# Attention and MLP on one core: the second MLP product by Strassen's scheme for eight of nine chunks of 512 tokens

## The chip, the core and the metric

The kernel runs on one core of a Trainium2 chip. The metric is the device time of one execution in microseconds (us); lower is better. Engines are named as in the profile: PE is TensorE (matmuls), PEld its weight loads, DVE VectorE, ACT ScalarE, POOL GpSimd, SP the sync engine, whose queue issues most DMAs.

## What is computed

The reference is attention over 8 batches of 8 heads (576 tokens, head size 64), in which scores more than tau below the maximum of their row are dropped, followed by an MLP on the 4608 tokens of 512 features:

```python
def _moe_ref(x, w_in, w_out) -> np.ndarray:
    h = x @ w_in
    sp = np.where(h > 20.0, h, np.log1p(np.exp(np.minimum(h, 20.0))))
    g = h * np.tanh(sp)
    return (g @ w_out).astype(np.float32)
```

`w_in` is 512 x 2048, `w_out` 2048 x 512. The gate h * tanh(softplus(h)) is one ACT instruction (Mish). The change concerns `g @ w_out`, the second product.

## The kernel before, in words

Matmuls take float32r operands, and each full-precision operand is split in two: an upper half (a copy into float32r, by ACT) and a lower half (the operand minus that copy, by DVE or POOL). A product is the sum of three matmuls: upper x upper, upper x lower, lower x upper. The weights arrive as 64-bit words and are decoded (class `Decode`): two conversions on ACT (`first`), clamp, shift and sign on DVE, `add` on POOL, then the upper half on ACT and the lower on DVE or POOL.

The first part of `attention_moe` (to line 655) runs attention tile by tile, with the first MLP product (`gemm1`) of the batch before it mixed in. `gemm1` takes 384 matmuls of 288 tokens a batch, in units of 12 that fill one PSUM bank (128 rows of h, 288 tokens); a copy by ACT or DVE takes each out, and four go to DRAM (`hd`) in one DMA.

Lines 657 to 799 are the first product of the last batch, 32 units (`u`). Beside it the first quarter of `w_out` is decoded in pieces of 256 columns (`PACE`), and h of the first tokens is loaded and gated (`GATES`, `GATES1`).

From line 800 on is the second product. Tokens go in chunks: 256, eight of 512, and 256. For each chunk and each 128 of the 512 output features (`d`), 48 matmuls with the chunk's tokens as moving columns run into one PSUM bank: 16 blocks of 128 hidden rows (`f`), three matmuls each (line 851). DVE copies the bank out (line 854), SP stores it (line 855). `make_g` makes the operand of the next chunk in pieces of 1024 elements: load, Mish (line 679), upper half on ACT (line 683), lower half on DVE (line 684). The rest of `w_out` is decoded during the first two chunks.

Every engine gets its instructions in the order in which the program makes them.

## Time and profile before

| | us |
|---|---|
| median of 3 runs | 1372.05 (1371.4 to 1372.26) |
| the profiled execution: its span | 1370.5 |
| second product, first matmul to end of span | 968.4 to 1370.5 |

The span is the time from the first to the last instruction of one profiled execution; the median of the runs is 1.55 us above it. In a group's row stand line, engine, operation, output<-input, shapes, count, busy time in all and mean ns of one, and behind the last bar the engine's idle time ahead of them and who ended it. A timeline row has start, duration, engine, line, operation; in brackets the idle time before it and the engine waited for. Line 94 is a helper that records operations, so names of tiles tell them apart there.

### The profile page before, as it was taken

To read this page: it belongs to the slowest core of one execution; us is meant where nothing else is said; L and a number is where in the kernel's file an instruction comes from. 1 tells how busy PE (TensorE), PEld (TensorE's weight loads), DVE (VectorE), ACT (ScalarE), POOL (GpSimd) and SP (SyncE) were. 2 spreads that over 40 slices of the span, in tenths; PEclk is the share of its full clock that TensorE was granted. 3 is DMA by queue.
4 is the path that set the end of the run, shared out by engine and by line. 5 is a ranking of instruction groups with operands and counts; after the bars stand their busy time and mean duration, and the time that the engine had idled before them with its cause. 6 is when DMAs were issued, how large, how long until landed. Compare 5 with 4: busy or idle time off the path is not lost.

```text
span 1370.5 us, 27694 instructions
## 1 busy us (share of the span) xinstructions
PE 1352.6 (99%) x8839; PEld 1225.3 (89%) x8839; DVE 1001.6 (73%) x2976; ACT 943.0 (69%) x2106; POOL 771.8 (56%) x1115
## 2 busy tenths in 40 slices
PE   9998899999999999999999999999999999999999
PEld 7555889999999999999999999999887888888888
DVE  6999999999999999999999999957874332232210
ACT  5878788888888888888888888856555543443210
POOL 5778888778788787887887878633460000000000
PEclk9999999999999999999999999999999999999999
DMA  5333323333333233332332323128655553543310
GB/s 152 98 98 107 114 80 114 108 96 103 101 99 115 89 120 93 111 107 97 103 112 88 124 90 110 60 88 277 196 164 151 153 148 102 143 131 102 93 52 23
DMA packets 126017, 154.64 MB, mean 113 GB/s; under 512 B 23472, under 2 KB 109488, under 8 KB 125872
## 3 DMA queue, kind: packets, MB, share of 16 engines
q1 hardware_dynamic: 124720, 148.16, 36.1%
q10 hardware_dynamic: 1152, 4.72, 0.9%
q8 instruction: 70, 1.15, 0.4%
q14 instruction: 75, 0.61, 0.1%
HBM read 105.64 MB, written 47.19 MB: 112 GB/s over the span
## 4 chain that ended last, share of the span: by engine, by line
PE 84%; DVE 5%; ACT 4%; DMA 2%; issue 2%; POOL 2%; SPq 1%; ACTq 0%; DVEq 0%; POOLq 0%
PE h L94 25%; PE o L851 23%; PE s L94 13%; PE y L94 12%; PE tp L94 9%; PE t L94 1%; DVE st L94 1%; DVE g L94 1%; DVE p L94 1%; DVE dec L94 1%; POOL w2l L157 1%; DMA ht<-hd 1%; DMA g<-hd 1%; ACT e L94 1%; DMA g<-w_out 1%
## 5 line engine op out<-in xcount | busy, mean ns | idle before, releaser
L851 PE MATMUL o<-g,w2h 128*128 128x512 f32 (+1 forms) x1280 | 363.9, 370 | 0.8 <-DVE g L684 0.8
L94 PE MATMUL h<-xh,w1h 128*128 128x288 f32 x1024 | 302.8, 296 | 1.1 <-ACT hst L94 0.6
L94 PE MATMUL h<-xh,w1l 128*128 128x288 f32 x1024 | 302.6, 296 | 0.0
L94 PE MATMUL h<-xl,w1h 128*128 128x288 f32 x1024 | 302.6, 295 | 0.0
L94 POOL TENSOR_SCALAR p<-p,st 128x576 f32<-128x576 f32 x288 | 243.8, 846 | 58.2 <-DVE st L94 33.8
L851 PEld LDWEIGHTS o<-g,w2h 128*128 128x128 f32 x1280 | 231.7, 188 | 43.7 <-DVE g L684 1.1
L94 PE MATMUL s<-k,q 128*128 128x288 f32 (+1 forms) x1280 | 255.2, 324 | 8.2 <-DVE p L94 7.9
L94 DVE SCALAR_TENSOR_TENSOR p<-s,st,e 128x576 f32<-128x576 f32 x288 | 235.1, 816 | 20.5 <-ACT e L94 11.0
L94 ACT ACTIVATE e<-s,st 128x576 f32<-128x576 f32 x288 | 214.2, 744 | 36.0 <-DVE st L94 30.4
L851 PE MATMUL o<-g,w2l 128*128 128x512 f32 (+1 forms) x640 | 236.2, 369 | 0.0
L94 DVE TENSOR_REDUCE st<-s 128x1 f32<-128x576 f32 x288 | 216.7, 752 | 2.6 <-PE s L94 2.5
L94 PEld LDWEIGHTS s<-k,q 128*128 128x128 f32 (+1 forms) x1280 | 182.7, 190 | 38.1 <-DVE p L94 23.6
L94 DVE TENSOR_TENSOR lo<-tp,hi 128x512 fp32r<-128x512 f32 (+1 forms) x280 | 174.7, 632 | 49.2 <-ACT hi L94 42.5
L94 PEld LDWEIGHTS h<-xh,w1h 128*128 128x128 f32 x1024 | 193.1, 189 | 1.9 <-ACT hst L94 1.1
L94 PEld LDWEIGHTS h<-xh,w1l 128*128 128x128 f32 x1024 | 193.0, 188 | 0.0
L94 PEld LDWEIGHTS h<-xl,w1h 128*128 128x128 f32 x1024 | 192.9, 188 | 0.0
L94 PE MATMUL tp<-ident,p 128*128 128x128 f32 x1152 | 174.4, 274 | 3.3 <-DVE lo L94 2.1
L94 ACT CAST hi<-tp 128x512 fp32r<-128x512 f32 (+1 forms) x280 | 149.7, 545 | 36.1 <-PE tp L94 33.1
L684 DVE TENSOR_TENSOR g<-ht,g 128x1024 fp32r<-128x1024 f32 (+1 forms) x60 | 68.6, 1153 | 137.0 <-ACT g L683 137.0
L94 PEld LDWEIGHTS tp<-ident,p 128*128 128x128 f32 x1152 | 138.9, 140 | 13.4 <-issue 5.4
L679 ACT ACTIVATE ht<-ht 128x1024 f32<-128x1024 f32 (+1 forms) x60 | 60.2, 1003 | 115.5 <-DMA ht<-hd 111.0
L851 PEld LDWEIGHTS o<-g,w2l 128*128 128x128 f32 x640 | 120.3, 188 | 21.3
(87 smaller groups left out, 2223.0 us busy)
## 6 DMA issues: line engine op xcount, KB each, us to landing
hd<-hst SPq DMA_DIRECT2D x56, 576.0 KB, 3.4
r<-q SPq DMA_DIRECT2D x120, 160.0 KB, 2.3
r<-k SPq DMA_DIRECT2D x120, 160.0 KB, 2.3
ht<-hd SPq DMA_DIRECT2D x52, 288.0 KB, 3.2
r<-v SPq DMA_DIRECT2D x56, 160.0 KB, 2.3
dec<-w_in SPq DMA_DIRECT2D x32, 256.0 KB, 2.8
out_t<-ost SPq DMA_DIRECT2D x32, 256.0 KB, 2.9
g<-w_out SPq DMA_DIRECT2D x48, 128.0 KB, 3.0
```

What stands on the lines that cost most here:

```text
L94: made = method(*args, **kwargs)
L157: engine.tensor_tensor(self.lo, fv(self.a), fv(self.hi), ALU.subtract)
L679: nc.scalar.activation(ht, ht, AF.Mish)
L684: engine.tensor_tensor(gl, ht, fv(gh), ALU.subtract)
L851: nc.tensor.matmul(o[:, :m], a, b, start=n == 0, stop=n == 3 * NF - 1)
```

## The change

The first 512 tokens (chunk 0) are multiplied as before, but with all four output blocks open at once: 8 groups, one for each pair of hidden blocks (j and j + 8), of 24 matmuls with 512 columns. The other 4096 tokens go in eight chunks of 512 by Strassen's scheme in Winograd's form. The output of a chunk is a 2 x 2 block matrix (two halves of the features, two of the tokens), as is each pair of hidden blocks; seven products of quarter size take the place of eight. A chunk has 8 groups of 7 products x 2 x 3 = 42 matmuls of 256 columns, in seven PSUM banks. So there are 72 groups (`NG`), numbered n; group n of chunk c is j = n - 8c.

- `load_z` loads h of a group (two DMAs), four quarters of 256 tokens.
- `combine` applies Mish (ACT, 1024 elements) and, for Strassen's chunks, makes three more quarters: one subtraction of 512 elements on DVE, then two of 256 on POOL, the second of which needs the first.
- `split_z` makes the upper half `gh` (ACT) and the lower half `gl` (DVE) of the seven quarters, 1792 elements each. `gh` and `gl` have three buffers.
- `sums_w` and `split_w` make the sums of the weight's quarters for chunks 1 to 8, beside chunk 0's matmuls.
- `leave` adds the seven products into four output quarters: one copy on ACT and seven additions on DVE out of PSUM, and four stores.
- `compose`, `upper_w`, `lower_w` decode the weight in pieces of 1024 elements, all of it beside the last batch of the first product, a piece every 4 units.
- h lies in DRAM in blocks of 256 tokens, so each store of it (`store`) is two DMAs; three weight loads and conversions move into the last steps of attention. The buffers of the first weight's decode, and the DMA scratch, are placed anew.

Its core, cut:

```diff
+        def compose(j):
...
+            nc.vector.tensor_scalar(fv(b), fv(top), TOP_MAX, -TOP_MAX, ALU.min, ALU.max)
+            nc.vector.tensor_scalar(a, b, 3, 0x7FFFFFF8, ALU.logical_shift_left, ALU.bitwise_and)
+            nc.vector.scalar_tensor_tensor(b, b, 0x80000000, a, ALU.bitwise_and, ALU.bitwise_or)
+            nc.gpsimd.tensor_tensor(b, b, low, ALU.add)
...
+        def combine(n):
+            if n < NG:
+                y = z[n]
+                nc.scalar.activation(y[:, :4], y[:, :4], AF.Mish)
+                if n >= NJ:
+                    nc.vector.tensor_tensor(
+                        y[:, 4:6], y[:, :1].to_broadcast([P, 2, QT]), y[:, 1:3], ALU.subtract
+                    )
+                    nc.gpsimd.tensor_tensor(y[:, 6], y[:, 1], y[:, 5], ALU.subtract)
+                    nc.gpsimd.tensor_tensor(y[:, 7], y[:, 6], y[:, 3], ALU.subtract)
+
+        def split_z(n):
+            if n < NG:
+                home = homes[("er", "wl", "wl")[n % 3]]
+                gs[n] = [home.tile([P, 7, QT], F32R, name=f"g{m}", tag=f"g{m}{n % 3}") for m in "hl"]
+                y = z[n][:, :4] if n < NJ else z.pop(n)[:, 1:]
+                to = [x[:, :4] if n < NJ else x for x in gs[n]]
+                nc.scalar.copy(to[0], y)
+                nc.vector.tensor_tensor(to[1], y, fv(to[0]), ALU.subtract)
...
+                    if NT <= g < NT + 3:
+                        convert(g - NT)
...
-                ost = wl.tile([P, NC], F32, name="ost", bufs=2)
-                nc.vector.tensor_copy(ost[:, :m], o[:, :m])
-                nc.sync.dma_start(out[d * P:(d + 1) * P, CHUNKS[c]:CHUNKS[c + 1]], ost[:, :m])
...
+        for n in range(NG):
+            c, j = divmod(n, NJ)
+            if n < NJ:
+                sums_w(n)
+            for i in range(n + 1 + (n > NJ + 1), n + 2 + (n > NJ)):
+                split_z(i)
+            if n < NJ:
+                split_w(n)
+            for i in range(n + 2 + (n > NJ), n + 3 + (n >= NJ)):
+                if i > 2:
+                    combine(i)
+            for i in range(n + 3 + (n >= NJ), n + 4 + (n >= NJ - 1)):
+                if i > 4:
+                    load_z(i)
...
+            for k, (wi, gi) in enumerate(PRODUCTS):
+                o = banks[k].rearrange("p (n t) -> p n t", t=QT)
+                w, at = (wa[j], (0, 2, 3)[wi]) if wi < 3 else (ws[j], wi - 3)
+                for b in range(2):
+                    cols = slice(at * QT + b * P, at * QT + (b + 1) * P)
+                    for i, (x, y) in enumerate(((0, 0), (0, 1), (1, 0))):
+                        nc.tensor.matmul(
+                            o[:, b], w[x][:, cols], gs[n][y][:, gi],
+                            start=j == b == i == 0, stop=j == NJ - 1 and b == 1 and i == 2,
+                        )
+                if j == NJ - 1:
+                    leave(k, c, o)
```

The order that this makes of DVE's queue in the steady part. Before, between two output copies (`ost`), DVE has only lower halves of 1024 elements, each of which waits for ACT's upper half:

```order
L684 TENSOR_TENSOR g_17501<-ht_17509,g_17501 128x1024
L684 TENSOR_TENSOR g_17516<-ht_17517,g_17516 128x1024
L684 TENSOR_TENSOR g_17516<-ht_17524,g_17516 128x1024
L854 COPY ost_17595<-o_17546 128x512
L684 TENSOR_TENSOR g_17531<-ht_17532,g_17531 128x1024
```

Now, at the end of a Strassen chunk (`z` written at 512 elements is the subtraction of `combine`, `c` the additions of `leave`):

```order
L91 TENSOR_TENSOR gl_16692<-z_16593,gh_16691 128x1792
L91 TENSOR_TENSOR z_16646<-z_16646 128x512
L91 TENSOR_TENSOR gl_16745<-z_16646,gh_16744 128x1792
L91 TENSOR_TENSOR z_16699<-z_16699 128x512
L91 TENSOR_TENSOR c_16769<-o_16374,c_16761 128x512
L91 TENSOR_TENSOR c_16777<-o_16375,c_16769 128x512
L91 TENSOR_TENSOR c_16785<-o_16376,c_16777 128x512
L91 TENSOR_TENSOR c_16769<-o_16376,c_16769 128x512
L91 TENSOR_TENSOR c_16769<-o_16377,c_16769 128x512
L91 TENSOR_TENSOR c_16777<-c_16777,o_16378 128x512
L91 TENSOR_TENSOR c_16761<-o_16379,c_16761 128x512
L91 TENSOR_TENSOR gl_16814<-z_16699,gh_16813 128x1792
```

The subtraction of a group stands behind `gl` of the group before it and ahead of its own `gl`; seven additions stand between the two once a chunk. ACT's queue there, with the engines whose semaphores each instruction waits for in brackets:

```order
L91 ACTIVATE z_16593<-z_16593 128x1024 [waits DMAHW6_49,DMAHW5_49]
L91 CAST gh_16691<-z_16593 128x1792 [waits DVE_49,PE_49,Pool_49]
L91 ACTIVATE z_16646<-z_16646 128x1024 [waits DMAHW7_49,DMAHW0_49]
L91 CAST gh_16744<-z_16646 128x1792 [waits DVE_49,PE_49,Pool_49]
L91 ACTIVATE z_16699<-z_16699 128x1024 [waits DMAHW2_49,DMAHW1_49]
```

`gh` of a group now waits for POOL's two subtractions, on an engine that has nothing to do in this part of the kernel before. The second place is DVE's queue from the end of the last first-product batch into chunk 0. Before, decoding and gating alternate with copies of h in small pieces:

```order
L94 TENSOR_TENSOR g_15361<-ht_15407,g_15360 128x1024
L94 COPY hst_15555<-h_15591 128x288
L94 TENSOR_SCALAR g_15359<-g_15359 128x256 x2
L94 SCALAR_TENSOR_TENSOR g_15359<-g_15359 128x256
```

Now the last piece of the weight (`w2l7`), the sums of its first piece and `gl` of group 1 (`gl_16025`):

```order
L91 TENSOR_SCALAR s_15941<-w_15747 128x1024
L91 TENSOR_SCALAR a_15940<-s_15941 128x1024
L91 SCALAR_TENSOR_TENSOR s_15941<-s_15941,a_15940 128x1024
L91 COPY hst_15962<-h_15949 128x288
L91 COPY hst_15962<-h_15980 128x288
L91 TENSOR_TENSOR w2l7_15994<-s_15941,w2h7_15939 128x1024
L91 TENSOR_TENSOR z_15766<-s_15414 128x256 x2
L91 TENSOR_TENSOR z_15766<-z_15766,s_15414 128x256
L91 TENSOR_TENSOR z_15766<-s_15414,z_15766 128x256
L91 TENSOR_TENSOR gl_16025<-z_15792,gh_16024 128x1024
```

The operand of chunk 0's second group stands behind the whole decode of the weight, which before lay partly beside the first two chunks.

## Prediction

> **What bounds the kernel now.** I read the page first: how long each engine is busy, and the chain that ended last.

> ```profile
> span 1370.5 us, 27694 instructions
> PE 1352.6 (99%) x8839; PEld 1225.3 (89%) x8839; DVE 1001.6 (73%) x2976; ACT 943.0 (69%) x2106; POOL 771.8 (56%) x1115
> PE 84%; DVE 5%; ACT 4%; DMA 2%; issue 2%; POOL 2%; SPq 1%; ACTq 0%; DVEq 0%; POOLq 0%
> ```

> TensorE (PE) is busy 99% of the span and owns the chain, so only fewer or cheaper matmuls shorten this kernel, as long as they are fed. Next the busy time by stage: attention's end, the start of the second product, and its steady part (columns: window, length, PE, weight loads, DVE, ACT, POOL, granted clock, DMA share, GB/s).

> ```profile
> 903.00:911.00 8.00, 8.00 (x62) 7.95 (x61) 2.72 (x7) 4.42 (x12) 1.88 (x3) 1.00 0.18 74
> 968.40:1026.00 57.60, 57.60 (x347) 51.31 (x346) 46.56 (x76) 31.92 (x74) 35.88 (x44) 1.00 0.51 156
> 1026.00:1370.50 344.50, 340.47 (x1577) 282.35 (x1575) 92.80 (x99) 120.26 (x123) 0.00 (x0) 1.00 0.39 110
> ```

> In the steady part DVE works 27% and ACT 35%, POOL not at all: there the other engines only convert the hidden values ahead of PE. The table of PE's waits has one wait in the whole second product:

> ```profile
> PE o L851 <- DVE g L684: 0.8, 1, 0.8
> ```

> The pace of the matmuls is read from when results leave (a matmul's own duration overlaps its neighbours'). Timeline of PE at the product's start, and of DVE near its end:

> ```profile
> 968.41 0.40 PE L851 MATMUL o<-g,w2h 128*128 128x256 f32 x2
> ...
> 1333.69 0.69 DVE L854 COPY ost<-o 128x512 f32<-128x512 f32 x1 [10.29 <-PE o L851]
> 1344.68 0.69 DVE L854 COPY ost<-o 128x512 f32<-128x512 f32 x1 [10.30 <-PE o L851]
> ...
> 1367.26 0.42 DVE L854 COPY ost<-o 128x256 f32<-128x256 f32 x1 [5.26 <-PE o L851]
> ```

> 48 matmuls of 512 columns take 10.99 us, 0.229 us each. The last 192, of 256 columns, take 22.58 us, 0.1176 each. Half the columns cost a little over half.

> **The matmuls: what the change saves.** Before, the product runs from 968.4 to 1367.3, 398.9 us. After, chunk 0 has 192 matmuls of 512 columns (43.9 us, 5.5 per group of 24), and each of eight chunks has 8 groups of 42 matmuls of 256: 4.94 us a group, 39.5 a chunk, 316.1 in all. Together 360.0: 38.9 us less, if PE never waits.

> [...]

> **The round that feeds a group.** Does PE stay fed? These groups of instructions have the forms that the new code uses (line, engine, operation, form, count, busy, mean ns):

> ```profile
> L684 DVE TENSOR_TENSOR g<-ht,g 128x1024 fp32r<-128x1024 f32 x52 | 63.2, 1224 | 124.1 <-ACT g L683 124.1
> L684 DVE TENSOR_TENSOR g<-ht,g 128x512 fp32r<-128x512 f32 x8 | 5.5, 692 | 12.9 <-ACT g L683 12.9
> L683 ACT CAST g<-ht 128x1024 fp32r<-128x1024 f32 x52 | 54.0, 1049 | 35.3 <-PE o L851 34.1
> L683 ACT CAST g<-ht 128x512 fp32r<-128x512 f32 x8 | 4.9, 620 | 12.4 <-PE o L851 12.2
> L679 ACT ACTIVATE ht<-ht 128x1024 f32<-128x1024 f32 x52 | 55.1, 1060 | 103.9 <-DMA ht<-hd 99.4 <-DVE ost L854 4.4
> L94 DVE TENSOR_TENSOR lo<-tp,hi 128x512 fp32r<-128x512 f32 x224 | 153.6, 686 | 40.1 <-ACT hi L94 34.8
> L94 POOL TENSOR_TENSOR k<-r,k 128x320 fp32r<-128x320 f32 x120 | 104.6, 877 | 9.9 <-ACT k L94 6.7
> ```

> Drawn out in a straight line to 1792 elements, ACT's upper half (gh) takes 1.049 + 768 x 0.838 ns = 1.69 us and DVE's lower half (gl) 1.224 + 768 x 1.04 ns = 2.02. The DVE subtraction of 512 takes 0.69, Mish 1.06. By engine a group costs ACT 2.75, DVE 2.71 and POOL about 1.5, each well under PE's 4.94. But they stand in one line. DVE's queue holds gl of group m, then the subtraction of m+1, then gl of m+1. The subtraction of m+1 therefore starts after gl of m; POOL's two need it; ACT's gh of m+1 needs POOL's; gl of m+1 needs gh. No two of these overlap, and each round makes one group.

> How much lies between engines is read from the timelines: DVE to POOL, POOL to ACT, ACT to DVE.

> ```profile
> 966.96 0.43 DVE L94 SCALAR_TENSOR_TENSOR g<-g 128x256 uint32<-128x256 uint32 x1
> 967.52 0.74 POOL L94 TENSOR_TENSOR g<-g 128x256 uint32<-128x256 uint32 x1 [4.18 <-DVE g L94]
> ...
> 943.37 0.81 POOL L94 TENSOR_TENSOR g<-g 128x256 uint32<-128x256 uint32 x1 [0.74 <-DVE g L94]
> 944.21 0.41 ACT L94 CAST w2h<-g 128x256 fp32r<-128x256 f32 x1 [1.14 <-POOL g L94]
> ...
> 963.72 1.05 ACT L94 CAST g<-ht 128x1024 fp32r<-128x1024 f32 x1
> 964.80 1.23 DVE L94 TENSOR_TENSOR g<-ht,g 128x1024 fp32r<-128x1024 f32 x1 [2.35 <-ACT g L94]
> ```

> The hops are 0.13, 0.03 and 0.03; POOL's 256 elements take 0.74 to 0.81. The round: gl 2.02 (less 0.07 by which the next DVE instruction starts early, below) + 0.69 + 0.13 + 2 x 0.76 + 0.03 + 1.69 + 0.03 = 6.04. POOL's second subtraction waits for its first, which no row prices: 0 to 0.3. I take **6.1 us**, with ends of 5.75 (shorter POOL and DVE starts) and 6.5 (0.07 more at each of five handovers). That is more than 4.94, so once the lead is used up, PE waits 1.1 to 1.2 us in every group.

> Is DVE's order really kept? In the trace it is:

> ```profile
> 939.22 1.22 DVE L94 TENSOR_TENSOR g<-ht,g 128x1024 fp32r<-128x1024 f32 x1 [4.53 <-ACT g L94]
> 940.37 0.45 DVE L94 COPY hst<-h 128x288 f32<-128x288 f32 x1
> ...
> 939.75 0.38 ACT L94 COPY hst<-h 128x288 f32<-128x288 f32 x1
> ```

> ACT's copy is of the bank that PE filled after the one that DVE copies here, and PE needs 12 matmuls for a bank, at least 1.4 us at 0.1176. So the bank of DVE's copy was full by 938.3, while DVE idled (4.53 us, until 939.22) for the instruction queued ahead of that copy. The copy then started 1.15 after an instruction of 1.22: the 0.07 above. [...]

> **Chunk edges.** At the end of a chunk seven DVE additions out of PSUM (0.69 each, as lo<-tp,hi; 4.8, with waits on each other 4.9) are queued between the subtraction and gl. 3.4 us of that lies beside POOL and gh; **1.5** is added, at seven edges 10.5 (0.8 to 2.6 each). Products of the next chunk wait for the banks that the additions empty (0.7 + 4.9 + 0.7 = 6.3 us after gl of its second group), so its first group ends late; but gh of three groups further, which overwrites that group's tiles, is due two rounds and the 1.5 less gl and gh after the same moment, 10 us, so this goes no further. On SP's queue four output DMAs stand ahead of the next load.

> ```profile
> L855 SPq DMA_DIRECT2D out_t<-ost x40: 332/351/467, 1013.8 to 1367.7; - x40
> ```

> They delay it by 4 x 0.35 = 1.4 us behind the last addition; it lands some 3 us later and is wanted two rounds on: nothing, and 1.4 an edge if that cover is gone. Mish of a group lies beside gl of the group before (1.06 of 2.02), its loads four rounds ahead: nothing. The new places of buffers and scratch put no instruction on any queue.

> **Entry.** The decode of the weight now goes by 1024 elements: clamp, shift and sign on DVE, add on POOL, upper on ACT, lower on DVE, with the next clamp behind the lower.

> ```profile
> 917.60 1.57 POOL L94 TENSOR_TENSOR xl<-x,xh 128x288 fp32r<-128x288 f32 x2 [0.55 <-ACT xh L94]
> 945.60 0.69 DVE L94 CAST g<-g 128x1024 fp32r<-128x1024 f32 x1 [1.67 <-DMA ht<-hd]
> 943.15 0.42 DVE L94 TENSOR_TENSOR w2l<-g,w2h 128x256 fp32r<-128x256 f32 x1
> ```

> By the POOL rows (0.74 at 256, 0.877 at 320) its 1024 take 2.35. A turn: clamp 0.69 to 1.2 (strided input, unseen), shift 0.69, sign 1.2, hop 0.13, add 2.35, upper 1.05, lower 1.15: 7.3 to 7.8, say 7.5. The first add waits for POOL's xl, done at 919.2; lower 0 ends at 923.8, two copies at 924.6, and seven turns later lower 7 at 977.1. Behind it stand four sums of 0.42 and gl of group 1: 980.0. PE wants that at 968.4 + 5.5 = 973.9: **6.1 us** of waiting (4 to 9). Then sums, gl and sl take DVE 4.1 us a group against 5.5, and PE runs free to the end of chunk 0. With eight PSUM banks in turn I expect no stop of PE inside the first product.

> **Attention.** Each store of h becomes two DMAs and three conversions of 2.1 us on ACT come into its last steps, where it works 4.4 of 8 us; their cover is that idle time, and an ACT copy that is late by one conversion can hold PE's bank up to about 1 us. I take 1, from -1 to 3.

> **The sum.** Chunk 0 ends at 968.4 + 1 + 43.9 + 6.1 = 1019.4. The lead, counted from there: DVE copies out the last bank (0.7), gl of 9 ends at 3.0, two subtractions at 4.2, POOL's pairs at 5.2 and 6.7, gh of 10 at 6.9, gl of 10 at 9.0 and of 11 at 11.0, and a round later that of 12 at 17.0. PE wants 9 to 12 at 4.9, 9.9, 14.8 and 19.8; at 1.2 us a group the lead is gone by group 15. gl of the last group, 59 rounds after group 12: 17.0 + 59 x 6.1 + 10.5 = 387.4, and 4.9 for its matmuls: 1411.7. The tail:

> ```profile
> out_t<-ost SPq DMA_DIRECT2D x32, 256.0 KB, 2.9
> out_t<-ost SPq DMA_DIRECT2D x8, 128.0 KB, 1.9
> ```

> From the last copy's start to the end it took 3.2; the last piece is now 256 KB (+1.0) and an addition of 0.69 for a copy of 0.42 (+0.3): 4.5. Span 1416.2. The median of the three runs, 1372.05, is 1.55 above the profiled span, so **1418 us**.

> **Rivals.** (1) PE stays the bound and the kernel is faster: a round under 4.94 us. 1418 - 387.4 - 4.9 + 316.1 = **1342**. It speaks for it that no engine's own work reaches 4.94; against it that all seven legs come from rows and stand in line. A round of 5.3 already equals 1372 ((1418 - 1372)/59 = 0.78 less). Chance 0.10.
> (2) PE's clock falls. It was granted 1.00 in every stage quoted, where PE was busy at least 98%; no row shows it with a wait in every group. At half clock a group takes 9.9 us, over the round, and the time is 1342 + 316 = **1658**. [...] Chance 0.04.

> **How the numbers follow.** The forecast has 0.86. The round's ends move it by 59 x -0.35 = -21 and 59 x 0.4 = +24, the other terms by 5 to 8 either way, less often together: 1395 to 1445, which leaves out both rivals and about 0.06 of the forecast. Within 0.2% (2.7 us, about what measurement can tell here) only a round of 5.3 ends: 0.01. Faster 0.10, slower 0.89.

> **What would show it.** Right: in the steady part gh starts every 6.1 us, DVE idles before gl for ACT and ACT before gh for POOL, PE's waits there are for gl and 70 to 80 us in sum (392 - 316), PE busy near 80%. Wrong: PE waits for nothing after chunk 0, or gh starts every 4.9 us; or a clock under 1.00 there.

## The result, and the profile after

The changed kernel takes **1421.8 us** (median of 4 runs, 1421.1 to 1421.8); the kernel before, beside it, 1372.0. The ratio is 1.0365 (95% interval 1.035 to 1.0381): slower by 50 us, 3.8 over the 1418 of the forecast and inside its range. The page of the profile after, its span, busy times and chain:

```profile
span 1420.0 us, 29648 instructions
PE 1345.4 (95%) x9799; PEld 1264.5 (89%) x9799; DVE 1102.4 (78%) x3018; ACT 990.0 (70%) x2052; POOL 837.0 (59%) x1191
issue 20%; POOL 6%; PE 3%; DVE 1%; ACT 0%; DMA 0%; POOLq 0%; DVEq 0%; ACTq 0%
```

The shares of the chain add up to 31% of the span: it was followed back to 979.7 us only, so it holds the second product alone and can't be set against the 84% of before as it stands. Of its 440 us PE has 40, nearly all in chunk 0; before, the last 321 us of matmuls were PE's in one piece. What owns the rest can't be read from this row: "issue" is the time that the chain could not give to anyone, here between POOL's pairs. The timelines show it. One round of the steady part (DVE, then POOL and ACT; the brackets have the wait and who ended it):

```profile
1099.59 2.02 DVE L91 TENSOR_TENSOR gl<-z,gh 128x1792 fp32r<-128x1792 f32 x1 [3.39 <-ACT gh L91]
1101.54 0.68 DVE L91 TENSOR_TENSOR z<-z 128x512 f32<-128x512 f32 x1
1105.60 2.03 DVE L91 TENSOR_TENSOR gl<-z,gh 128x1792 fp32r<-128x1792 f32 x1 [3.38 <-ACT gh L91]
...
1102.30 1.54 POOL L91 TENSOR_TENSOR z<-z 128x256 f32<-128x256 f32 x2 [4.46 <-DVE z L91]
...
1103.88 1.69 ACT L91 CAST gh<-z 128x1792 fp32r<-128x1792 f32 x1 [3.35 <-POOL z L91]
```

Follow the starts: gl 1099.59, subtraction 1101.54, POOL's pair 1102.30, gh 1103.88, gl of the next group 1105.60. Each begins within 0.1 us of the end of the one before it, none lies beside another, and the round is **6.01 us** (6.04 worked out, 6.1 taken). All three engines idle over half of it and none is late by its own work.

At a chunk edge the seven additions stand ahead of gl; it starts 7.32 us after the one before, 1.3 more than a round:

```profile
1123.61 2.02 DVE L91 TENSOR_TENSOR gl<-z,gh 128x1792 fp32r<-128x1792 f32 x1 [3.35 <-ACT gh L91]
...
1126.15 3.67 DVE L91 TENSOR_TENSOR c<-o,c 128x512 f32<-128x512 f32 x5
...
1130.93 2.01 DVE L91 TENSOR_TENSOR gl<-z,gh 128x1792 fp32r<-128x1792 f32 x1
```

PE's longest waits (what it waited for, sum in us, times, longest; all lie in the steady part but one of the 19 for gl, 0.5 us at the entry), and the window of the steady part (length, PE, weight loads, DVE, ACT, POOL, clock, DMA share, GB/s):

```profile
PE o L91 <- ACT c L91: 31.4, 7, 4.5
PE o L91 <- DVE gl L91: 12.3, 19, 0.8
```

```profile
1050.00:1410.00 360.00, 315.46 (x2471) 308.31 (x2469) 184.97 (x166) 157.10 (x124) 85.05 (x116) 0.93 0.32 100
```

That is not the picture that the forecast drew: PE is busy 88%, not 80%, its largest wait is for a PSUM bank at the chunk's edge and not for gl, and the granted clock is 0.93. A table of waits read alone would name the banks. The experiments ask whether PE, its clock or its banks have any part in the 50 us.

### The profile page after: what moved, and what is told of

It is laid out like the page before. It is cut to its first block, busy times and chain, and to the rows that moved or that the text cites. A ratio compares the mean times of both kernels' runs of the same rounds, so it can differ in the third digit from the quotient of the medians.

```text
span 1420.0 us, 29648 instructions
## 1 busy us (share of the span) xinstructions
PE 1345.4 (95%) x9799; PEld 1264.5 (89%) x9799; DVE 1102.4 (78%) x3018; ACT 990.0 (70%) x2052; POOL 837.0 (59%) x1191
## 5 line engine op out<-in xcount | busy, mean ns | idle before, releaser
L91 POOL TENSOR_TENSOR z<-z 128x256 f32<-128x256 f32 x128 | 94.3, 737 | 332.1 <-DVE z L91 319.9
L91 DVE TENSOR_TENSOR gl<-z,gh 128x1792 fp32r<-128x1792 f32 (+1 forms) x72 | 140.7, 1956 | 191.6 <-ACT gh L91 191.5
L91 ACT CAST gh<-z 128x1792 fp32r<-128x1792 f32 (+1 forms) x72 | 116.4, 1619 | 224.5 <-POOL z L91 210.1
L91 DVE SCALAR_TENSOR_TENSOR p<-s,st,e 128x576 f32<-128x576 f32 x288 | 235.0, 816 | 20.3 <-ACT e L91 10.5
L91 PE MATMUL o<-gh,sh 128*128 128x256 f32 x512 | 152.6, 298 | 32.7 <-ACT c L91 31.4
L91 PE MATMUL o<-gh,sl 128*128 128x256 f32 x512 | 150.8, 294 | 0.0
L91 PE MATMUL o<-gl,sh 128*128 128x256 f32 x512 | 150.5, 294 | 0.0
## 6 DMA issues: line engine op xcount, KB each, us to landing
z<-hd SPq DMA_DIRECT2D x144, 256.0 KB, 3.1
out_t<-c SPq DMA_DIRECT2D x36, 256.0 KB, 2.4
dec<-w_in SPq DMA_DIRECT2D x32, 256.0 KB, 3.4
```

Source lines behind the costliest of these rows:

```text
L91: made = method(*args, **kwargs)
```

## Experiments

The theory is that of the forecast: the serial round sets the pace after chunk 0, and PE waits on it. The main rival: PE itself is slower in the groups of 42 matmuls, by its lower clock or by twice as many weight loads. Two smaller questions are the late entry and what is left once the round is broken. Times are medians; ratios are to the kernel before, run beside each of them (1371.4 us for e1 to e4, 1372.2 for e5 to e8).

**e1, the order alone.** Two emissions change places, from group 12 on:

```diff
+            if n > NJ + 1:
+                combine(n + 3)
             for i in range(n + 1 + (n > NJ + 1), n + 2 + (n > NJ)):
                 split_z(i)
...
-                if i > 2:
+                if i > 2 and n <= NJ + 1:
                     combine(i)
```

> Order alone is changed, from group 12 on: Mish and the subtractions of group n+3 are put in the queues ahead of gh and gl of group n+2; the same instructions, the same numbers. Theory (the serial round sets the time): POOL's pair of one group now lies beside gh and gl of the group before, no instruction waits a whole round, and the matmuls bind again: gh starts every 4.9 to 5.1 us, chunk 0 still ends near 1029, and 1029 + 316 + 4.5 + 1.8 gives 1351 us (1345 to 1365). Rival (TensorE itself is slower in the Strassen groups, by its clock of 0.93 or by twice as many weight loads): the order doesn't matter to it, and the time stays above 1400.

Measured: **1353.3 us**, ratio 0.987 (0.9857 to 0.9884). The same instructions with the same operands in another order are 68 us faster, and 1.3% faster than the kernel before. Steady part, and PE's longest wait after attention, which lies at the entry:

```profile
1050.00:1340.00 290.00, 290.00 (x2460) 290.00 (x2459) 192.06 (x164) 154.40 (x121) 115.12 (x116) 1.00 0.40 124
```

```profile
PE o L91 <- ACT gh L91: 6.2, 1, 6.2
```

PE is busy all 290 us at a clock of 1.00; the bank waits and the lower clock went with the round, though nothing was done about either. They were its consequences. The rival falls.

**e2, a third of the matmuls left out** in chunks 1 to 8, those of the weight's lower half:

```diff
-                    for i, (x, y) in enumerate(((0, 0), (0, 1), (1, 0))):
+                    for i, (x, y) in enumerate(((0, 0), (0, 1))):
...
-                            start=j == b == i == 0, stop=j == NJ - 1 and b == 1 and i == 2,
+                            start=j == b == i == 0, stop=j == NJ - 1 and b == 1 and i == 1,
```

> The third matmul of each product (lower half of the weight x upper half of the activations) is left out in chunks 1 to 8: 28 matmuls in a group in place of 42, 3.3 us in place of 4.94. Theory: the round stays 6.01, only the last group's matmuls are shorter (1.6 us): 1416 to 1422 us, and TensorE waits about 2.7 us in each group. Rival (TensorE sets the pace): a third of its time goes, 100 us less, 1320 us.

Measured: **1421.6 us**, ratio 1.0368 (1.0354 to 1.0382), 0.2 us from the changed kernel. Its steady window and DVE's gl:

```profile
1050.00:1340.00 290.00, 205.55 (x1319) 190.26 (x1317) 149.68 (x136) 127.06 (x101) 68.96 (x94) 0.83 0.34 107
```

```profile
1099.90 2.03 DVE L91 TENSOR_TENSOR gl<-z,gh 128x1792 fp32r<-128x1792 f32 x1 [3.39 <-ACT gh L91]
...
1105.92 2.02 DVE L91 TENSOR_TENSOR gl<-z,gh 128x1792 fp32r<-128x1792 f32 x1 [3.39 <-ACT gh L91]
```

896 matmuls less and a clock of 0.83 change nothing, and the round is 6.02. Of TensorE's time in this stage a third is worth nothing.

**e3, POOL's pair on DVE.** A leg of the round made shorter:

```diff
-                    nc.gpsimd.tensor_tensor(y[:, 6], y[:, 1], y[:, 5], ALU.subtract)
-                    nc.gpsimd.tensor_tensor(y[:, 7], y[:, 6], y[:, 3], ALU.subtract)
+                    nc.vector.tensor_tensor(y[:, 6], y[:, 1], y[:, 5], ALU.subtract)
+                    nc.vector.tensor_tensor(y[:, 7], y[:, 6], y[:, 3], ALU.subtract)
```

> POOL's two subtractions of 256 go to DVE, where they stand behind its own of 512; order otherwise kept. Theory: out of the round go 1.54 and two hops (0.16), in come two instructions of 0.42: 6.01 becomes 5.2, 59 x 0.81 = 48 us less. At a chunk edge the additions now have only gh (1.7) beside them and not POOL's pair too: 1.8 more at each of seven edges, 12 us. 1386 us (1375 to 1396). Rival (TensorE is the bound at its lower clock): DVE has more work and nothing is gained, 1415 or more.

Measured: **1396.6 us**, ratio 1.0186 (1.0172 to 1.02): 25 us less, where 36 were expected; it misses the range by 0.6.

```profile
1099.92 2.02 DVE L91 TENSOR_TENSOR gl<-z,gh 128x1792 fp32r<-128x1792 f32 x1 [1.83 <-ACT gh L91]
1101.86 1.60 DVE L91 TENSOR_TENSOR z<-z 128x512 f32<-128x512 f32 x3
1105.30 2.02 DVE L91 TENSOR_TENSOR gl<-z,gh 128x1792 fp32r<-128x1792 f32 x1 [1.83 <-ACT gh L91]
```

The round is 5.38, not 5.2: the three subtractions take 1.60 where I had 1.53, and I left out the hop from DVE to ACT (0.12). 59 x 0.63 = 37 less, and 7 x 1.6 = 11 given back at the edges (gl is now 8.24 us apart there, 2.86 over a round, against 1.3): 26. A busier DVE made the kernel faster because it had the shorter leg.

**e5, a leg made longer.** POOL's second subtraction is written twice:

```diff
                     nc.gpsimd.tensor_tensor(y[:, 7], y[:, 6], y[:, 3], ALU.subtract)
+                    nc.gpsimd.tensor_tensor(y[:, 7], y[:, 6], y[:, 3], ALU.subtract)
```

> The changed kernel with POOL's second subtraction written twice, the same numbers into the same place: one more instruction of 0.77 in the round. Theory: every round is 0.77 to 0.8 longer, 6.8 in all; 59 rounds add 45 to 47, and at the edges the additions have 0.77 more beside them, 7 x 0.77 = 5 less: 1421.8 + 41 = 1463 us (1458 to 1469). Rival (POOL's work lies beside TensorE's or ACT's): under 5 us more.

Measured: **1466.6 us**, ratio 1.0691 (1.0673 to 1.0709), 44.8 more.

```profile
1100.84 2.03 DVE L91 TENSOR_TENSOR gl<-z,gh 128x1792 fp32r<-128x1792 f32 x1 [4.20 <-ACT gh L91]
...
1107.68 2.03 DVE L91 TENSOR_TENSOR gl<-z,gh 128x1792 fp32r<-128x1792 f32 x1 [4.21 <-ACT gh L91]
...
1103.55 2.37 POOL L91 TENSOR_TENSOR z<-z 128x256 f32<-128x256 f32 x3 [4.46 <-DVE z L91]
```

The round is 6.84, 0.83 more; 59 x 0.83 = 49, less 6 at the edges, which POOL now covers longer (gl is 7.33 apart there, 0.5 over a round, against 1.3), and 2 more before group 12: 45. So rounds of 5.38, 6.01 and 6.84 us give 1396.6, 1421.8 and 1466.6: the time follows the round in both directions, on an engine that is busy a quarter of it.

**e4, the entry.** The changed kernel with the decode's first DVE steps put ahead of the lower half of the piece before:

```diff
-                steps.setdefault(u, []).append((compose, j))
+                steps.setdefault(max(u - 2, 0), []).append((compose, j))
```

> The first three DVE steps of each piece of the second weight (compose) are put two units earlier, ahead of the lower half of the piece before it; nothing else moves. Theory on the entry (a turn of 7.5 us in one line, with ACT blocked by it, stopped TensorE inside the first product and before group 1): a turn falls to about 5 us, the decode keeps up with the first product, TensorE's stops of 0.4, 0.9 and 3.4 us go and the wait before group 1 shrinks to 3 or 4: 6 to 9 us less, 1413 to 1416. Rival (the entry is late because the conversions in attention's last steps delay the chain there, or because the clock was 0.75 in that stretch): 0 to 2 us less.

Measured: **1413.2 us**, ratio 1.0311 (1.0297 to 1.0325), 8.6 less. PE's stops at the entry of the changed kernel, and two windows of its clock there:

```profile
961.99 0.40 PE L91 MATMUL h<-xh,w1h 128*128 128x288 f32 x1 [0.43 <-DVE hst L91]
967.93 0.40 PE L91 MATMUL h<-xh,w1h 128*128 128x288 f32 x1 [0.88 <-ACT hst L91]
973.16 0.77 PE L91 MATMUL o<-gh,w2h 128*128 128x512 f32 x1 [3.37 <-ACT hst L91]
986.68 0.80 PE L91 MATMUL o<-gh,w2h 128*128 128x512 f32 x1 [5.04 <-ACT gh L91]
987.94 0.80 PE L91 MATMUL o<-gl,w2h 128*128 128x512 f32 x1 [0.47 <-DVE gl L91]
```

```profile
972.00:976.00 4.00, 2.84 (x7) 2.32 (x8) 3.93 (x7) 2.44 (x4) 0.00 (x0) 0.53 0.57 151
988.00:992.00 4.00, 4.00 (x10) 3.13 (x11) 3.97 (x7) 2.01 (x3) 0.00 (x0) 0.50 0.41 126
```

And with the decode ahead: the second product's first matmul, its one long stop, and the end of chunk 0.

```profile
968.20 0.40 PE L91 MATMUL o<-gh,w2h 128*128 128x512 f32 x1
...
977.79 0.79 PE L91 MATMUL o<-gh,w2h 128*128 128x512 f32 x1 [3.94 <-ACT gh L91]
...
1019.75 0.69 DVE L91 COPY c<-o 128x512 f32<-128x512 f32 x1 [2.11 <-PE o L91]
```

The product starts at 968.2 and not 973.2, chunk 0 ends, by the start of the copy of its last bank, at 1019.8 and not 1029.1. After it the round is unchanged. ACT's queue in the changed kernel shows how a decode that PE doesn't wait for stopped it:

```profile
964.17 1.05 ACT L91 CAST w2h<-s 128x1024 fp32r<-128x1024 f32 x1 [1.45 <-POOL s L91]
...
967.50 0.38 ACT L91 COPY hst<-h 128x288 f32<-128x288 f32 x1
...
971.85 0.41 ACT L91 COPY hst<-h 128x288 f32<-128x288 f32 x1
...
979.72 1.05 ACT L91 CAST w2h<-s 128x1024 fp32r<-128x1024 f32 x1 [3.16 <-POOL s L91]
...
982.04 0.93 ACTq L91 DMA_DIRECT2D hd<-hst  x2
985.58 1.04 ACT L91 CAST gh<-z 128x1024 fp32r<-128x1024 f32 x1 [3.57 <-DMA hd<-hst]
```

ACT stands still for POOL's add of a piece, and then has 10 us of work with one gap of 1.0, with the copies that empty PE's banks in between: PE stood 0.88 us for the copy at 967.50. The next add holds ACT again at 979.72, and so the last store of h, issued at 982.04. The stop of 3.37 is put down to ACT's copy at 971.85, but that one ended at 972.26, and PE's weights start to load 0.87 later. The rows around it (DVE, POOL, PEld):

```profile
969.95 2.73 DVE L91 TENSOR_TENSOR gl<-z,gh 128x1024 fp32r<-128x1024 f32 x1 [0.89 <-ACT gh L91]
972.61 0.44 DVE L91 COPY hst<-h 128x288 f32<-128x288 f32 x1
...
969.20 2.40 POOL L91 TENSOR_TENSOR s<-s,w 128x1024 uint32<-128x1024 uint32 x1 [5.07 <-DVE s L91]
...
973.13 0.29 PEld L91 LDWEIGHTS o<-gh,w2h 128*128 128x128 f32 x1 [3.58 <-ACT hst L91]
```

PE starts 0.07 after DVE's copy has ended, here and in the four other runs with this entry (e1, e2, e3, e5). That copy stands behind gl of group 0, which waited for a late gh and then took 2.73 us in place of 1.22, beside POOL's add (last section). So about 1.5 of the 3.37 (an estimate, 2.73 - 1.22) comes from this meeting of DVE and POOL; in e4 this gl ran alone, in 1.21.

The row at 985.58 shows what is left in e4 as well (3.94): gh of group 1 goes into a pool that lies over the first product's buffers, and waits until the last store of h has landed. Another place for it was not tried.

**e6, both edits** (e1 and e4).

> The swapped order of e1 and the earlier decode of e4 together. Theory: they act at different places (the round after chunk 0, the entry before it), so that their gains add up: 1353.3 - 8.6 = 1344.7 us (1342 to 1347), close to the 1342 that rival (1) of the prediction worked out for matmuls that never wait. Rival (what e4 gained at the entry was only lead that the long round used up; where matmuls bind, a part of it is lost): 1348 to 1353.

Measured: **1344.1 us**, ratio 0.9795 (0.9781 to 0.981), 28 us faster than the kernel before. The gains add up (1353.3 - 8.6 = 1344.7). PE's longest wait in the second product, the only one but for 0.5 us right behind it, is now

```profile
PE o L91 <- ACT gh L91: 3.9, 1, 3.9
```

**e7, e6 with POOL's pair on DVE** (the edit of e3).

> As e6, with POOL's two subtractions on DVE. In e1 POOL's pairs took up to 5.1 us for four where DVE's gl ran beside them, against 1.54 for two alone. If the matmuls bind and these two engines have room, nothing changes: within 1.5 us of e6 (DVE then has 0.69 + 0.92 + 2.02 = 3.6 us a group and 0.6 of the edge, under 4.94). Rival (the pairs stretched by DVE are what is left over the 1342 of fed matmuls): 3 us or more less than e6.

Measured: 1344.5 us, ratio 0.9801 (0.9786 to 0.9815), no different from e6. Once no round is closed, it doesn't matter which engine has the pair: the edit that was worth 25 us in the round is worth nothing outside it.

**e8, e6 with the three conversions out of attention:**

```diff
-                    if NT <= g < NT + 3:
-                        convert(g - NT)
...
+            for j, u in enumerate((0, 1, 4)):
+                steps[u] = [(convert, j)] + steps.get(u, [])
```

> As e6, but the conversions of the first three pieces of the second weight are taken out of attention's last steps and put into the first steps of the last batch's first product. If they are what delayed attention's end (its last copies came 1.4 us later than in the kernel before): 1 to 2 us less than e6. If they lay beside TensorE's work: within 0.5 us of e6. More, if the decode, which starts later, then comes too late for group 1: 1 to 3 us more.

Measured: 1344.5 us, ratio 0.9797 (0.9782 to 0.9812), the same. Attention's last copies come 2.2 us earlier than in e6 (its row is first), and the second product begins that much earlier (966.5 for 968.6), but the stop before group 1 grows from 3.9 to 4.8, and the end doesn't move by what these runs can tell.

```profile
918.99 0.77 ACT L91 CAST xh<-x 128x288 fp32r<-128x288 f32 x2 [0.85 <-POOL x L91]
```

```profile
916.81 0.77 ACT L91 CAST xh<-x 128x288 fp32r<-128x288 f32 x2 [0.84 <-POOL x L91]
```

## Why the prediction was right, and where it was off

The mechanism held. By its own steps, against the profiled spans (1416.2 forecast, 1420.0 measured):

- **The matmuls' saving**: right. In e1's steady window 2460 take 290 us, 0.118 us each (0.1176 taken), and e6's 1344.1 is 2 over the 1342 that the first rival gave for a PE that never waits. The change does save PE's time; it can't be had while the round is 6 us.
- **The round**: right, and the largest term. The 0 to 0.3 allowed for POOL's second subtraction behind its first was 0.07 (the page has 0.737 for one, and the pair takes 1.54, where the sum had 1.52). 59 x 0.09 = 5.3 us too much, because I took 6.1 over the 6.04 that the rows gave.
- **Edges**: 1.3 for 1.5, 1.5 us too much in all. The bank waits "go no further": right, since gl right behind an edge is again 6.01 apart.
- **Lead**: gl of group 12 ended 17.2 us after chunk 0 (17.0). **Last matmuls and tail**: 10.2 (9.4).
- **Entry**: this failed, by 9.6 us. Chunk 0 ended at 1029.0 and not 1019.4. The sentence that failed is "With eight PSUM banks in turn I expect no stop of PE inside the first product": it stopped for 0.43, 0.88 and 3.37, because the copies of ACT and DVE stood behind steps of the decode and of group 0's operand, so the product began at 973.2 (969.4 forecast, 3.8). The eight banks did not cover these three stops. The wait for group 1 was 5.5 (6.1), near by luck. In the forecast it ends with DVE, behind the last lower half at 977.1; that one ended only at 982.0, mostly since the first clamp, and not only the first add, waited for POOL's xl, until 920.6. But DVE had its sums done by 983.5 and idled 3.2 us more: the wait ended with gh on ACT, which waited for the landing of h's last store, and no step of the forecast has that. The rest, 6.5, lies in chunk 0's matmuls, 50.4 us without waits for 43.9: behind the two stops the clock was 0.50 for 5.9 and 6.0 us, and a matmul of 512 columns took about 0.43 and not 0.229, which is over 5 of the 6.5. The sum had nothing for the clock there. e4 shows what the blocked queue cost: chunk 0 ends 9.3 earlier and the time is 8.6 less. That it ends at 1019.8, near the 1019.4 of the forecast, is chance: there too the stop before group 1 waits for the store, and behind it chunk 0's matmuls take 47.1.
- **Attention**: +1 taken, about 0 in the sum. In e4, which leaves the conversions there, the second product starts 0.2 us earlier than before the change. The conversions are not free: without them it starts 2.2 earlier (e8), so other parts of the change must give as much back, which was not followed up; and the stop before group 1 takes up part of what they cost. Runs with the same code up to there differ by 1.3 us in this start (968.2 in e4, 969.5 in e7).

Sum: +9.6 + 0.2 - 5.3 - 1.5 + 0.8 = +3.8 on the span, and 1.8 from span to median (1.55 taken). So two errors, of the entry and of the round's rounding up, partly cancelled; the forecast's nearness is better than its parts.

**What would show it** was half wrong. "PE's waits there are for gl and 70 to 80 us in sum", PE busy near 80%, the clock at 1.00: the waits were 31 for banks and 12 for gl, PE was busy 88%, and the clock was 0.93. The slack of a chunk (8 x 1.07 + 1.3 = 9.9 us) was there, but at the edge PE took it in one piece:

```profile
1124.00:1128.00 4.00, 2.76 (x11) 2.47 (x12) 3.79 (x5) 1.12 (x3) 1.46 (x2) 0.50 0.32 79
1128.00:1132.00 4.00, 4.00 (x31) 4.00 (x31) 3.90 (x6) 2.53 (x2) 0.00 (x0) 0.85 0.64 221
1132.00:1136.00 4.00, 4.00 (x36) 4.00 (x36) 1.54 (x2) 0.80 (x1) 1.47 (x2) 1.00 0.73 228
```

It waits 4.5 us for ACT's copy, which stands behind a gh that waits for POOL; then it runs at half clock until about 1129, and then works off its backlog at full pace, without waiting, until the end of the chunk. Waits for gl show only there, in the chunk's last groups. Behind the seven stops the half clock lasted 38 us in all; the matmuls start 0.214 us apart there in place of 0.118, which uses up some 17 us of slack (an estimate, 38 x (1 - 0.118/0.214)) and counts as busy. I had followed who waits for the banks only to ask whether it reaches gh, and not what it does to PE's own rows.

The first rival (PE stays the bound) was the right picture of what the kernel does once the loop is broken: e6. Of the second rival (the clock at half) the drop is there, 0.50 behind each stop, but stays in the slack: e2 has a clock of 0.83 and no loss. It cost time only at the entry, where no lead covered it. At 0.50 a group would take 9.0 us (an estimate, 42 x 0.214), and not the 9.9 of the rival.

## What to carry to other kernels

When an operand passes from engine to engine and back, lay the queues' orders side by side and look for a round: the work of group m+1 that is queued behind the last step of group m. The round here cost the sum of its legs, 6.01 us, though every engine in it was idle for over half of it, and order alone broke it (e1, 68 us less): put the first step of the next group ahead of the last step of this one. A wait of PE that a table names, or a lowered clock, can be the mark of such a round and not its cause, as the bank waits of 31 us and the clock of 0.93 were here; leave a third of PE's work out, and the time tells (e2, 0.2 us). And where a table names who ended a wait, look when that one ended: at the entry it had been done for 0.87 us.

## What the runs showed of the hardware

**DVE beside POOL.** In e4 the lower half of a piece of the weight, which runs alone in the changed kernel, lies beside POOL's add (DVE, POOL; then the changed kernel's group):

```profile
954.14 3.37 DVE L91 TENSOR_TENSOR w2l<-s,w2h 128x1024 fp32r<-128x1024 f32 x1
...
953.98 2.44 POOL L91 TENSOR_TENSOR s<-s,w 128x1024 uint32<-128x1024 uint32 x1 [4.17 <-DVE s L91]
```

```profile
L91 DVE TENSOR_TENSOR w2l<-s,w2h 128x1024 fp32r<-128x1024 f32 x8 | 9.8, 1223 | 21.3 <-ACT w2h L91 21.3
```

It takes 3.37 for 1.22: it starts on time, and ends 1.1 after POOL's add has ended at 956.42. In e1 it is POOL that takes longer: four subtractions, 3.1 us alone (two pairs of 1.54), begin 0.17 behind a gl of 2.02 and take 5.12.

```profile
1112.73 2.02 DVE L91 TENSOR_TENSOR gl<-z,gh 128x1792 fp32r<-128x1792 f32 x1
...
1112.90 5.12 POOL L91 TENSOR_TENSOR z<-z 128x256 f32<-128x256 f32 x4 [8.16 <-DVE z L91]
```

In the changed kernel's round none of the legs overlaps another, so this played no part there; at the entry gl of group 0 took 2.73 beside POOL's add, and 1.21 without it (e4, above). In e6 there is room for it: e7, which has no pair on POOL, takes 1344.5 us for 1344.1.

```profile
1142.11:1145.52 3.41, 1.23 (x8) 0.83 (x7) 2.26 (x2) 2.08 (x2) 0.00 (x0) 1.00 0.02 7
1145.52:1148.93 3.41, 3.41 (x17) 3.41 (x18) 0.37 (x1) 1.39 (x1) 1.47 (x2) 0.50 0.54 155
```

```profile
1143.28 0.38 PE L91 MATMUL o<-gh,w2h 128*128 128x256 f32 x1 [0.50 <-ACT gh L91]
1145.34 0.45 PE L91 MATMUL o<-gl,w2h 128*128 128x256 f32 x1 [1.68 <-DVE gl L91]
```

Here both waits lie in one window, in which PE idles 2.18 of the 3.41 us, and the next window runs at half clock. Two groups later the same two waits (0.48 before 1155.30 and 1.68 before 1157.36) lie in two windows, with 0.56 and 1.60 us of idle time, and the clock stays at 1.00. So in the windows quoted the drops went with the idle time that fell into one window (2.18 us and more against 1.60 and less), and not with the length of one wait. This is read from the records of these two runs alone; no run was made to try it.
